# Queries and keys handed over head dimension first in a fused attention and two-layer feed-forward kernel

## The chip, the cores and the metric

The kernel runs on one core of a Trainium2 chip. The metric is device microseconds (us) of one execution. Five engines work at once, each in the order of its own queue: TensorE (PE for its matmuls, PEld for its weight loads), VectorE (DVE), ScalarE (ACT), GpSimd (POOL) and SyncE (SP), which here only issues transfers. Matmul results land in PSUM banks, everything else lives in SBUF.

## The reference, cut to what matters

```python
# q, k, v: (8 batches, 8 heads, 576 positions, 64)
k_p = k.reshape(B, H, 72, 8, 64).mean(axis=3)      # groups of 8 keys are averaged
v_p = v.reshape(B, H, 72, 8, 64).mean(axis=3)
scores = scale * q @ k_p.T                         # 576 x 72 for each head
attn = softmax(scores)
x = (attn @ v_p), heads side by side               # 4608 tokens x 512
x = (h * cos(h)) @ moe_w_out,              h = x @ moe_w_in      # 512 -> 2048 -> 512
x = (g * clip(g + 3, 0, 6) / 6) @ moe2_w_out, g = x @ moe2_w_in
```

## The kernel before

**Attention.** Work is cut into 40 units: 8 batches by 5 units of 128 query rows (the fifth has 64). Heads go in four pairs, so that a pair fills 128 partitions (2 x 64). The keys of a batch are loaded key group by key group (`load_kv`, tile `raw`, one buffer that keys and values share), pooled on DVE with two halvings (L413) and a last addition that is done twice, side by side (L417, tile `kp`). `make_kbd` turns `kp` around with five TensorE transposes (four at L427, one at L443) into a PSUM piece, and five ACT copies (L424) put the result into `kbd`, an operand with the two heads of a pair on its block diagonal; there are two of these, for odd and even batches. A unit's queries are loaded row by row (`load_q`, tile `qm`, four buffers) and turned around in `unit_q` with four transposes (L472) and one ACT copy (L474) into `qT`. Then `unit_s` multiplies `qT` by `kbd`, half of the heads at a time (L486), DVE takes the row maxima (L495) and subtracts them (L497), ACT takes exponentials (L502), DVE and POOL normalise (L508 to L514), `unit_pt` transposes the weights on TensorE (L538), and `pv` multiplies by the pooled values (L573) and stores to `x_d`.

**PSUM.** Attention's PSUM results are "pieces" (`piece`). Up to the point where the first batch's output is complete, scores use the ring `ap` (two buffers), the turned queries and keys use the banks `h`, and the rest uses the banks `y`. After that, every kind of piece takes turns in the ring `ap`.

**First feed-forward layer.** Its 4608 tokens go in nine blocks of 512. A step is one block by one chunk of hidden units: `gemm1` (12 matmuls, L281), a chain of ACT and DVE operations, and two steps later `gemm2` (12 matmuls, L324). x arrives from `x_d` and is split by ACT and POOL (L258, L259). The scores of the first nine units come before any step; the rest is interleaved with the steps. `attention()` is a generator, and each `yield` ends one piece of work; how many pieces have been taken by each half step is fixed by a formula of `base`, `PACE` and the table `GOFF`, and a scheduler orders each engine's queue from that. The last scores are computed near 420 us; then come the rest of the first layer and the second layer (L900).

```python
            if n < units:
                unit_s(n, 0)
                yield
                unit_s(n, 1)
                unit_exp(n)
                yield
```

Of the kernel before, what the change touches and what calls it, by code (L numbers as in the profile page):

```python
# [8 lines left out]
F32 = mybir.dt.float32  # L9
# [3 lines left out]
AF = mybir.ActivationFunctionType  # L13
ALU = mybir.AluOpType
# [4 lines left out]
POOL = 8  # L19
# [9 lines left out]
@with_exitstack  # L29
def tile_kernel(ctx, tc, q, k, v, wi1, wo1, wi2, wo2, ident_d, mask_d, out):  # L30
    nc = tc.nc
    B, H, S, D = q.shape
    DM, NT = out.shape
    P = 128
    N = 512
    SP = S // POOL
    NP = H // 2
# [11 lines left out]
    K0S = 5  # L49
# [6 lines left out]
    KD = [0, 1, 1, 1, 1, 1, 1, 1]  # L56
    VD = [1, 0, 1, 1, 1, 1, 1, 1]
# [6 lines left out]
    KC = (H * SP + P - 1) // P  # L64
    KFULL = (H * SP) // P
    KREM = H * SP - KFULL * P
    UNITS = [(n0, min(P, S - n0)) for n0 in range(0, S, P)]
    NU = len(UNITS)
# [276 lines left out]
    ap = actx.enter_context(tc.tile_pool(name="ap", bufs=1))  # L345
    ps_a = actx.enter_context(tc.tile_pool(name="ps_a", bufs=2, space=PSUM))

    ident = ap.tile([P, P], F32, name="ident")
# [3 lines left out]
    raw, kp = {}, {}  # L352
    kbd = [ap.tile([P, NP, 2 * SP], F32, name=f"kbd{n}") for n in range(2)]
# [3 lines left out]
    qm, qT, pts = {}, {}, {}  # L357
# [7 lines left out]
    def piece(kind):  # L365
        turn = turns[kind] = turns.get(kind, -1) + 1
        if started:
            return ps_a.tile([P, N], F32, tag="ap", name="ap_ps", bufs=2)
        tag = SKIND[kind][turn % len(SKIND[kind])]
        if tag == "ap":  # L370
            return ps_a.tile([P, N], F32, tag="ap", name="ap_ps", bufs=2)
        if tag == "h":
            return ps_h.tile([P, N], F32, tag="h", name="h")
        return ps_y.tile([P, N], F32, tag=tag, name=tag)

    def load_kv(b, nm, step=KFULL):
        src = {"k": k, "v": v}[nm][b].rearrange("h (s r) d -> (h s) (r d)", r=POOL)
        if nm == "v":
            pairs = src.rearrange("(j x) e -> x j e", x=2 * SP)
            nc.sync.dma_start(out=raw_t[:, :NP, :], in_=pairs[:P])  # L380
            for half in range(2):
                o = half * NP * VR
                nc.sync.dma_start(
                    out=raw_t[o : o + NP * VR, NP, :],
                    in_=src.rearrange("(j x) e -> j x e", x=2 * SP)[:, P:],
                )
            return
        for c in range(0, KFULL, step):
            nc.sync.dma_start(
                out=raw_t[:, c : min(c + step, KFULL), :],  # L390
                in_=src[c * P : min(c + step, KFULL) * P, :].rearrange("(c p) e -> p c e", p=P),
            )
        nc.sync.dma_start(out=raw_t[:KREM, KFULL, :], in_=src[KFULL * P :, :])

    def load_q(n):
        b, i = divmod(n, NU)
        n0, w = UNITS[i]
        t = ap.tile([P, H * D], F32, tag="qm", name="qm", bufs=4)
        nc.sync.dma_start(
            out=t[:w].rearrange("p (h d) -> p h d", d=D),  # L400
            in_=q[b, :, n0 : n0 + w, :].rearrange("h p d -> p h d"),
        )
        qm[n] = t

    def pool_kv(b, nm, eng, step=KC):
        kt = ap.tile([P, KC, 2, D], F32, tag="kp", name="kp") if nm == "k" else None
        vt = ap.tile([P, KC, D], F32, tag="vt", name="vt") if nm == "v" else None
        for c in range(0, KC, step):
            t = raw_t[:, c : min(c + step, KC)]
            w = POOL * D  # L410
            while w > 2 * D:
                w //= 2
                eng.tensor_tensor(  # L413
                    out=t[:, :, :w], in0=t[:, :, :w], in1=t[:, :, w : 2 * w], op=ALU.add
                )
            for o in [kt[:, c : min(c + step, KC), e] for e in range(2)] if nm == "k" else [vt[:, c : min(c + step, KC)]]:
                eng.tensor_tensor(out=o, in0=t[:, :, :D], in1=t[:, :, D : 2 * D], op=ALU.add)  # L417
        kp[b, nm] = kt if nm == "k" else vt

    def make_kbd(b, part):  # L420
        kt = kp[b, "k"]
        ps = piece("q")
        kb = kbd[b % 2]
        cp = lambda o, i_: nc.scalar.activation(out=o, in_=i_, func=AF.Copy)  # L424
        if part == 0:
            for c in range(KFULL):
                nc.tensor.transpose(  # L427
                    ps[:, c * P : (c + 1) * P], kt[:, c].rearrange("p e d -> p (e d)"), ident
                )
            full = (KFULL * P) // (2 * SP)  # L430
            cp(
                kb[:D, :full, :SP],
                ps[:D, : full * 2 * SP].rearrange("p (j x) -> p j x", x=2 * SP)[:, :, :SP],
            )
            cp(
                kb[D:, :full, SP:],
                ps[D:, : full * 2 * SP].rearrange("p (j x) -> p j x", x=2 * SP)[:, :, SP:],
            )
            o = full * 2 * SP
            cp(kb[:D, full, :SP], ps[:D, o : o + SP])  # L440
            cp(kb[D:, full, SP : KFULL * P - o], ps[D:, o + SP : KFULL * P])
        else:
            nc.tensor.transpose(  # L443
                ps[:, :KREM], kt[:KREM, KFULL].rearrange("p e d -> p (e d)"), ident[:KREM, :KREM]
            )
            cp(kb[D:, NP - 1, 2 * SP - KREM :], ps[D:, :KREM])

    def make_v(b):
        vt = kp.pop((b, "v"))
# [6 lines left out]
        for x, src, rows in (("h", f(sp_h), P), ("l", sp_l, half)):  # L456
# [7 lines left out]
                in1=rest[:rows].to_broadcast([rows, NP, D]),  # L464
                op=ALU.mult,
            )

    def unit_q(n):
        w = UNITS[n % NU][1]
        ps = piece("q")  # L470
        for j in range(NP):
            nc.tensor.transpose(ps[:, j * P : j * P + w], qm[n][:w, j * P : (j + 1) * P], ident[:w, :w])  # L472
        t = ap.tile([P, NP, P], F32, tag="qT", name="qT", bufs=2)
        nc.scalar.activation(  # L474
            out=t[:, :, :w], in_=ps.rearrange("p (j n) -> p j n", n=P)[:, :, :w], func=AF.Copy
        )
        qT[n] = t
        del qm[n]

    def unit_s(n, half):  # L480
        b, i = divmod(n, NU)
# [104 lines left out]
    def attention():  # L586
        units = B * NU
        normed = finished = 0
        for n in range(units + 3):
            b, i = divmod(n, NU)  # L590
# [6 lines that stand above are left out]
                if n + 3 < units:  # L597
                    load_q(n + 3)
                if n + 1 < units:
                    unit_q(n + 1)  # L600
                    yield
            if n < units and b + 1 < B:
                if i == 2:
                    pool_kv(b + 1, "k", nc.vector if KD[b + 1] else nc.gpsimd)
                    load_kv(b + 1, "v")
                if i == 4:
                    make_kbd(b + 1, 0)
                    yield
                    make_kbd(b + 1, 1)
                    yield  # L610
            while normed < units and n - normed >= NL[normed // NU]:
                unit_norm(normed)
                normed += 1
            while finished < normed and n - finished >= 2:
                unit_pt(finished)
                yield
                qb, qi = divmod(finished, NU)
                finished += 1
                if qi in (1, 3):
                    unit_pt_rest(qb, qi - 1)  # L620
                    yield
                for part, (u0, u1) in enumerate(PARTS[qb]):
                    if qi == min(u1 - 1 + (part == 0) * PV0, NU - 1):
                        for j in range(NP):
                            pv(qb, part, j)
                            yield
                        if UNITS[u1 - 1][0] + P >= N:
                            started.append(qb)
                if qi == NU - 1:
                    done.append(qb)  # L630
                    if qb + 1 < B:
                        pool_kv(qb + 1, "v", nc.vector if VD[qb + 1] else nc.gpsimd)
                        make_v(qb + 1)
                        if qb + 2 < B:
                            load_kv(qb + 2, "k")
# [9 lines left out]
        steps += [(0, (1, bl), bl, fc, fc == n, fc == NF - 1) for fc in range(n, NF)]  # L645
    SB = len(steps)

    load_kv(0, "k", KFULL if K0S > KFULL else K0S)
    nc.sync.dma_start(out=ident, in_=ident_d)
    for n in range(3):  # L650
        load_q(n)
    nc.vector.memset(raw_t[KREM:, KFULL, :], 0.0)
    for n in range(2):
        nc.vector.memset(kbd[n], 0.0)
    nc.sync.dma_start(out=mask[:, : 2 + NP], in_=mask_d)
    for t in vr.values():
        nc.gpsimd.memset(f(t), 0.0)
    pool_kv(0, "k", nc.vector, K0S)
    load_kv(0, "v")
    make_kbd(0, 0)  # L660
    make_kbd(0, 1)
    unit_q(0)
    pool_kv(0, "v", nc.vector if VD[0] else nc.gpsimd)
    make_v(0)
    load_kv(1, "k")
    att = attention()
# [441 lines left out]
```

## Time and profile before

| | us |
|---|---|
| median of three runs (lowest, highest) | 1718.68 (1715.75, 1719.0) |
| the profiled execution, its own time | 1720.11 |
| its span, first to last instruction | 1718.3 |
| PE busy in the span | 1648.3 |
| DVE busy | 1158.8 |
| ACT busy | 981.3 |
| POOL busy | 346.4 |

Busy time of PE counts overlapping matmuls once. The span is the profiled execution alone, so the sums of the prediction stand against 1720.11 us, and their difference is taken off the median.

### The profile page before, as it was taken

How to read it: one execution, taken by the hardware profiler on the slowest of the kernel's cores; microseconds unless marked ns; L12 is line 12 of the kernel's file. 1: busy time of each engine (PE TensorE's matmuls, PEld its weight loads, DVE VectorE, ACT ScalarE, POOL GpSimd, SP SyncE). 2: the span in 40 equal slices, each digit the busy share in tenths (PEclk: the TensorE clock that was granted, in tenths of full speed). 3: DMA queues.
4: the chain of work that ended last, by engine and by line, in shares of the span. 5: the costliest groups of instructions: out<-in, count | busy, mean ns of one | idle time of the engine just before them, and what ended most of it. 6: DMA issues, size and time to landing. Idle time of an engine off the chain costs nothing. (4 is left out here: it accounts for less than half of the span.)

```text
span 1718.3 us, 21588 instructions
## 1 busy us (share of the span) xinstructions
PE 1648.3 (96%) x7858; PEld 1368.2 (80%) x7858; DVE 1158.8 (67%) x1580; ACT 981.3 (57%) x1473; POOL 346.4 (20%) x266
## 2 busy tenths in 40 slices
PE   4789999999999999999999998999999999999999
PEld 3567777787888888888888788888888888888889
DVE  6999666656676888788887435353555576768665
ACT  3578887788666666666565434353444344444444
POOL 2756543232333201111104003020202000000000
PEclk8799999999999999999999998999999999999999
DMA  7756434321433367656566274243428955344231
GB/s 189 217 170 184 151 121 126 113 87 35 150 115 129 93 206 267 195 188 206 184 209 189 99 283 145 99 167 128 147 114 302 324 224 187 113 157 137 84 110 38
DMA packets 174857, 274.11 MB, mean 160 GB/s; under 512 B 48672, under 2 KB 95904, under 8 KB 174752
## 3 DMA queue, kind: packets, MB, share of 16 engines
q1 hardware_dynamic: 174752, 272.75, 48.3%
q8 instruction: 62, 1.02, 0.3%
q14 instruction: 43, 0.35, 0.1%
HBM read 167.84 MB, written 104.86 MB: 159 GB/s over the span
## 5 line engine op out<-in xcount | busy, mean ns | idle before, releaser
L900 PE MATMUL bank<-wa,wb 128*128 128x512 f32 (+1 forms) x1368 | 292.8, 362 | 5.7 <-issue 4.1
L900 PEld LDWEIGHTS bank<-wa,wb 128*128 128x128 f32 x1368 | 235.4, 193 | 44.2 <-issue 4.2
L324 PE MATMUL y<-gh,wb 128*128 128x512 f32 x648 | 211.8, 391 | 0.0
L281 PE MATMUL h<-xh,wb 128*128 128x512 f32 x648 | 211.6, 390 | 0.2 <-ACT xh L258 0.2
L752 ACT ACTIVATE wa<-wu 128x1024 fp32r<-128x1024 f32 (+1 forms) x130 | 127.5, 981 | 142.7 <-PE bank L900 124.4
L900 PE MATMUL bank<-wu,wb 128*128 128x512 f32 (+1 forms) x792 | 198.4, 386 | 0.0
L294 DVE SCALAR_TENSOR_TENSOR g<-g,t 128x512 f32<-128x512 f32 x144 | 116.4, 809 | 102.4 <-ACT g L293 101.8
L281 PE MATMUL h<-xh,wa 128*128 128x512 f32 x504 | 175.0, 404 | 0.0
L259 POOL TENSOR_TENSOR xl<-xr,xh 128x512 fp32r<-128x512 f32 x72 | 107.6, 1508 | 324.0 <-ACT xh L258 323.3
L900 PEld LDWEIGHTS bank<-wu,wb 128*128 128x128 f32 x792 | 148.8, 188 | 29.9
L324 PE MATMUL y<-gh,wa 128*128 128x512 f32 x504 | 169.6, 396 | 0.0
L324 PEld LDWEIGHTS y<-gh,wb 128*128 128x128 f32 x648 | 122.4, 189 | 25.5
L281 PEld LDWEIGHTS h<-xh,wb 128*128 128x128 f32 x648 | 121.6, 188 | 25.6 <-ACT xh L258 0.6
L297 ACT ACTIVATE g<-g 128x512 f32<-128x512 f32 x144 | 91.1, 633 | 72.3 <-DVE g L294 71.9
L304 ACT ACTIVATE gh<-g 128x512 fp32r<-128x512 f32 x144 | 90.5, 629 | 68.7 <-DVE g L301 68.3
L281 PE MATMUL h<-xl,wb 128*128 128x512 f32 x324 | 126.3, 390 | 1.1 <-POOL xl L259 1.1
L753 DVE TENSOR_TENSOR wa<-wu,wa 128x1024 fp32r<-128x1024 f32 (+1 forms) x80 | 89.5, 1124 | 55.3 <-ACT wa L752 55.2
L324 PE MATMUL y<-gl,wb 128*128 128x512 f32 x324 | 126.5, 390 | 0.0
L301 DVE TENSOR_TENSOR g<-h,g 128x512 f32<-128x512 f32 x144 | 98.8, 686 | 36.8 <-ACT g L297 36.6
L1011 ACT ACTIVATE wu<-bank,bias_c 128x1024 f32<-128x1024 f32 (+1 forms) x60 | 61.8, 1031 | 99.2 <-PE bank L900 85.4
L900 PE MATMUL bank<-wa,wa 128*128 128x512 f32 (+1 forms) x552 | 117.5, 359 | 0.0
L288 ACT ACTIVATE t<-h 128x512 f32<-128x512 f32 x144 | 84.9, 590 | 52.8 <-PE h L281 52.3
(174 smaller groups left out, 3101.4 us busy)
## 6 DMA issues: line engine op xcount, KB each, us to landing
g_d<-wu SPq DMA_DIRECT2D x64, 512.0 KB, 2.6
wu<-g_d SPq DMA_DIRECT2D x56, 512.0 KB, 4.5
xr<-x_d SPq DMA_DIRECT2D x72, 256.0 KB, 3.3
wb<-s_d SPq DMA_DIRECT2D x36, 512.0 KB, 5.0
s_d<-wa SPq DMA_DIRECT2D x32, 512.0 KB, 3.7
s_d<-wa SPq DMA_DIRECT2D x32, 384.0 KB, 4.5
yp_d<-ys SPq DMA_DIRECT2D x36, 256.0 KB, 2.3
yv<-yp_d SPq DMA_DIRECT2D x36, 256.0 KB, 3.5
```

Source lines behind the costliest of these rows:

```text
L259: nc.gpsimd.tensor_tensor(out=xl, in0=t, in1=f(xh), op=ALU.subtract)
L281: nc.tensor.matmul(h, a[:, cs], z, start=(n == 0), stop=(n == 3 * NC - 1))
L288: nc.scalar.activation(out=t, in_=hs[s], func=AF.Copy, bias=0.25, scale=INV_2PI)
L294: mark[s] = nc.vector.scalar_tensor_tensor(out=g, in0=g, scalar=MAGIC, in1=t, op0=ALU.subtract, op1=ALU.subtract)
L297: nc.scalar.activation(out=g, in_=g, func=AF.Sin, scale=-TWO_PI)
L301: nc.vector.tensor_tensor(out=g, in0=hs[s], in1=g, op=ALU.mult)
L304: nc.scalar.activation(out=gh, in_=g, func=AF.Copy)
L324: nc.tensor.matmul(y[c], a, z, start=(first and n == 0), stop=(last and n == 2))
L752: nc.scalar.activation(out=hi, in_=src, func=AF.Copy)
L753: el.tensor_tensor(out=lo, in0=src, in1=f(hi), op=ALU.subtract)
L900: nc.tensor.matmul(bank[:, e, :wide], w[:, j, h, e], z[:, j], start=start and j == 0 and x == 0, stop=stop and j == 1 and x == 2, skip_gro ...
L1011: nc.scalar.activation(out=r, in_=c, func=AF.Relu, bias=bias_c[:, 2:3], scale=1.0)
```

## The change

The host hands over `q` as (batch, head pair, 2 x 64, 576) and `k` as (batch, 2 x 64, 8 x 4 x 72), with the position inside a key group outermost. So a query load lands directly as `qT`, now with four buffers, and `unit_q`, `qm` and the second tile are gone. The keys land with the head dimension on the partitions; `pool_k` halves them twice over 2304 elements (L407 of the new kernel) and does the last addition as two DVE operations of 64 partitions that write the two diagonal blocks of `kbd` (L411). `make_kbd` and `kp` are gone. The values' path, the number of yields and all pacing tables stay; a yield that ended a `unit_q` or `make_kbd` piece now ends an empty one. The reordering on the host is not part of the time.

```diff
-        for c in range(0, KFULL, step):
-            nc.sync.dma_start(
-                out=raw_t[:, c : min(c + step, KFULL), :],
-                in_=src[c * P : min(c + step, KFULL) * P, :].rearrange("(c p) e -> p c e", p=P),
-            )
-        nc.sync.dma_start(out=raw_t[:KREM, KFULL, :], in_=src[KFULL * P :, :])
+        flat = raw_t.rearrange("p c e -> p (c e)")
+        for c in range(0, POOL, step):
+            cs = slice(c * NP * SP, (c + step) * NP * SP)
+            nc.sync.dma_start(out=flat[:, cs], in_=k[b][:, cs])
...
-        t = ap.tile([P, H * D], F32, tag="qm", name="qm", bufs=4)
+        t = ap.tile([P, NP, P], F32, tag="qT", name="qT", bufs=4)
         nc.sync.dma_start(
-            out=t[:w].rearrange("p (h d) -> p h d", d=D),
-            in_=q[b, :, n0 : n0 + w, :].rearrange("h p d -> p h d"),
+            out=t[:, :, :w], in_=q[b, :, :, n0 : n0 + w].rearrange("j p n -> p j n")
         )
-        qm[n] = t
+        qT[n] = t
...
+    def pool_k(b, eng):
+        t = raw_t.rearrange("p c e -> p (c e)")[:, : POOL * NP * SP]
+        w = POOL * NP * SP
+        while w > 2 * NP * SP:
+            w //= 2
+            eng.tensor_tensor(out=t[:, :w], in0=t[:, :w], in1=t[:, w : 2 * w], op=ALU.add)
+        t = t.rearrange("p (r j x) -> p r j x", j=NP, x=SP)
+        kb = kbd[b % 2]
+        for e, p in enumerate((slice(0, D), slice(D, P))):
+            eng.tensor_tensor(
+                out=kb[p, :, e * SP : (e + 1) * SP], in0=t[p, 0], in1=t[p, 1], op=ALU.add
+            )
...
                 if n + 1 < units:
-                    unit_q(n + 1)
                     yield
             if n < units and b + 1 < B:
                 if i == 2:
-                    pool_kv(b + 1, "k", nc.vector if KD[b + 1] else nc.gpsimd)
+                    pool_k(b + 1, nc.vector)
                     load_kv(b + 1, "v")
                 if i == 4:
-                    make_kbd(b + 1, 0)
                     yield
-                    make_kbd(b + 1, 1)
                     yield
```

What that makes of the queues shows at three places. First, the beginning of PE's queue, before (`kp` pooled keys, `qm` queries as loaded, `e` the scores less their maxima, `y` a PSUM bank):

```order
L427 MATMUL h<-ident,kp 128x128 x4
L443 MATMUL h<-ident,kp 128x64
L472 MATMUL h<-ident,qm 128x128 x8
L486 MATMUL ap_ps<-kbd_104,qT 128x144 x4
L472 MATMUL h<-ident,qm 128x128 x4
L486 MATMUL ap_ps<-kbd_104,qT 128x144 x6
L538 MATMUL y_280<-ident,e_106 128x128
```

And the same place in the changed kernel, where scores are L452 and the transposes of the weights L504 and L526:

```order
L452 MATMUL ap_ps<-kbd_104,qT 128x144 x12
L504 MATMUL y_235<-ident,e_106 128x128 x4
L452 MATMUL ap_ps<-kbd_104,qT 128x144 x4
L504 MATMUL y_274<-ident,e_107 128x128 x4
L526 MATMUL y_281<-ident,e_106 128x128
```

The score matmuls of three units now stand first, with nothing of PE or ACT between the pooled keys and them. Second, the beginning of DVE's queue before, after its first memsets:

```order
L413 TENSOR_TENSOR raw<-raw 128x5x256
L413 TENSOR_TENSOR raw<-raw 128x5x128
L417 TENSOR_TENSOR kp<-raw 128x5x64 x2
L495 TENSOR_REDUCE mx<-ap_ps 128x4 x2
L497 TENSOR_TENSOR e_106<-ap_ps,mx 128x288 x2
L495 TENSOR_REDUCE mx<-ap_ps 128x4
L413 TENSOR_TENSOR raw<-raw 128x5x256
```

And in the changed kernel, where L407 and L411 pool the keys, L461 and L463 are the maxima and the subtraction, and L420 pools the values:

```order
L407 TENSOR_TENSOR raw<-raw 128x1152
L407 TENSOR_TENSOR raw<-raw 128x576
L411 TENSOR_TENSOR kbd_104<-raw 64x4x72 x2
L461 TENSOR_REDUCE mx<-ap_ps 128x4
L463 TENSOR_TENSOR e_106<-ap_ps,mx 128x288
L461 TENSOR_REDUCE mx<-ap_ps 128x4
L463 TENSOR_TENSOR e_106<-ap_ps,mx 128x288
L461 TENSOR_REDUCE mx<-ap_ps 128x4 x2
L463 TENSOR_TENSOR e_107<-ap_ps,mx 128x288 x2
L420 TENSOR_TENSOR raw<-raw 128x5x256
```

The first pooling of values stands behind three more operations of the second unit than before. Third, PE's queue in the middle of the interleaved part, at the same step of the first layer, before:

```order
L324 MATMUL y_1959<-gh,wa_928 128x512
L486 MATMUL ap_ps<-kbd_104,qT 128x144 x2
L324 MATMUL y_1959<-gl,wa_928 128x512
L486 MATMUL ap_ps<-kbd_104,qT 128x144 x2
L324 MATMUL y_1959<-gh,wa_929 128x512
L324 MATMUL y_1960<-gh,wa_928 128x512
L472 MATMUL ap_ps<-ident,qm 128x128 x4
L324 MATMUL y_1960<-gl,wa_928 128x512
```

And in the changed kernel:

```order
L324 MATMUL y_1741<-gh,wa_794 128x512
L452 MATMUL ap_ps<-kbd_104,qT 128x144 x2
L324 MATMUL y_1741<-gl,wa_794 128x512
L452 MATMUL ap_ps<-kbd_104,qT 128x144 x2
L324 MATMUL y_1741<-gh,wa_795 128x512
L324 MATMUL y_1742<-gh,wa_794 128x512
L504 MATMUL ap_ps<-ident,e_106 128x128 x4
L324 MATMUL y_1742<-gl,wa_794 128x512
```

The transposes of queries are gone, the step holds the same scores, and the transposes of the weights (before, four matmuls of L324 later) have moved up into their place in the ring `ap`.

## Rows read from the trace of the kernel before

**Rows 1.** The page, part 1: busy us (share of the span) and instructions.

```profile
PE 1648.3 (96%) x7858; PEld 1368.2 (80%) x7858; DVE 1158.8 (67%) x1580; ACT 981.3 (57%) x1473; POOL 346.4 (20%) x266
```

**Rows 2.** Windows, by stage: start:end, length, busy us by engine, granted clock, DMA share, GB/s.

```profile
20.00:80.00 60.00, 36.94 (x171) 29.01 (x172) 55.91 (x100) 28.52 (x61) 38.07 (x33) 0.72 0.74 202
80.00:160.00 80.00, 67.30 (x356) 52.35 (x355) 76.07 (x123) 63.85 (x118) 46.75 (x39) 0.98 0.60 176
160.00:420.00 260.00, 248.94 (x1320) 201.80 (x1319) 166.24 (x306) 211.71 (x362) 99.89 (x93) 1.00 0.36 110
420.00:1044.00 624.00, 617.78 (x2815) 514.34 (x2813) 457.48 (x681) 375.93 (x623) 116.81 (x79) 0.99 0.54 177
1044.00:1718.00 674.00, 669.78 (x3170) 564.50 (x3170) 396.08 (x357) 296.41 (x302) 43.68 (x18) 1.00 0.44 155
```

**Rows 3.** Groups by line, 0 to 620 us: count, busy us, mean ns, idle before.

```profile
L472 PE MATMUL ap_ps<-ident,qm 128*128 128x128 f32 (+1 forms) x128 | 19.1, 269 | 6.8 <-issue 6.7
L427 PE MATMUL ap_ps<-ident,kp 128*128 128x128 f32 x24 | 3.6, 272 | 0.0
```

**Rows 4.** Windows of line L472 alone (PE, PEld).

```profile
80.00:160.00 80.00, 4.33 (x28) 3.02 (x28) 0.98 0.60 176
160.00:420.00 260.00, 13.22 (x92) 10.07 (x92) 1.00 0.36 110
```

**Rows 5.** Windows of line L427 alone (PE, PEld).

```profile
160.00:420.00 260.00, 2.40 (x16) 1.88 (x16) 1.00 0.36 110
```

**Rows 6.** Timeline of PE near 193 us: start us, length us, what.

```profile
192.69 0.39 PE L281 MATMUL h<-xl,wa 128*128 128x512 f32 x1
192.93 0.60 PE L472 MATMUL ap_ps<-ident,qm 128*128 128x128 f32 x4
193.36 0.60 PE L427 MATMUL ap_ps<-ident,kp 128*128 128x128 f32 x4
193.72 0.48 PE L281 MATMUL h<-xh,wa 128*128 128x512 f32 x1
...
194.26 0.40 PE L324 MATMUL y<-gl,wa 128*128 128x512 f32 x1
194.59 0.27 PE L443 MATMUL ap_ps<-ident,kp 64*128 64x64 f32 x1
194.79 0.50 PE L324 MATMUL y<-gh,wa 128*128 128x512 f32 x1
```

**Rows 7.** Waits of PE, 160 to 420 us: total us, times, longest.

```profile
PE ap_ps L472 <- issue: 3.5, 3, 1.8
PE ap_ps L486 <- DVE pth L551: 2.0, 3, 1.1
PE h L281 <- POOL xl L259: 2.0, 3, 1.0
```

**Rows 8.** Timeline of the start, all engines, in brackets the idle time before.

```profile
7.57 2.35 DVE L413 TENSOR_TENSOR raw<-raw 128x1280 f32<-128x1280 f32 x2 [4.69 <-DMA raw<-in_k_dram]
9.96 0.90 DVE L417 TENSOR_TENSOR kp<-raw 128x320 f32<-128x320 f32 x2
10.88 0.37 SPq L380 DMA_DIRECT2D raw<-in_v_dram  x1
...
15.04 2.29 PE L486 MATMUL ap_ps<-kbd,qT 128*128 128x144 f32 x8
...
16.41 0.46 DVE L495 TENSOR_REDUCE mx<-ap_ps 128x4 f32<-128x288 f32 x1 [5.55 <-PE ap_ps L486]
...
20.92 1.49 DVE L413 TENSOR_TENSOR raw<-raw 128x1280 f32<-128x1280 f32 x1 [1.36 <-DMA raw<-in_v_dram]
```

**Rows 9.** Waits of DVE, 0 to 160 us.

```profile
DVE mx L495 <- PE ap_ps L486: 8.5, 5, 5.6
```

**Rows 10.** Windows 55:65 and 80:130, columns as in rows 2.

```profile
55.00:65.00 10.00, 6.66 (x26) 5.91 (x27) 9.90 (x21) 3.36 (x6) 7.18 (x7) 0.53 0.71 195
80.00:130.00 50.00, 40.78 (x217) 32.52 (x216) 48.51 (x77) 38.09 (x70) 26.93 (x23) 0.97 0.59 169
```

More of the change, by code (lines that the diff above doesn't have):

```diff
@@ L31, in tile_kernel @@
     nc = tc.nc
-    B, H, S, D = q.shape
+    B, H, S, D = v.shape
     DM, NT = out.shape
@@ L374, in piece, with load_kv @@
         return ps_y.tile([P, N], F32, tag=tag, name=tag)
-    def load_kv(b, nm, step=KFULL):
-        src = {"k": k, "v": v}[nm][b].rearrange("h (s r) d -> (h s) (r d)", r=POOL)
+    def load_kv(b, nm, step=POOL):
         if nm == "v":
+            src = v[b].rearrange("h (s r) d -> (h s) (r d)", r=POOL)
             pairs = src.rearrange("(j x) e -> x j e", x=2 * SP)
@@ L397, in load_q @@
         n0, w = UNITS[i]
-        t = ap.tile([P, H * D], F32, tag="qm", name="qm", bufs=4)
+        t = ap.tile([P, NP, P], F32, tag="qT", name="qT", bufs=4)
         nc.sync.dma_start(
-            out=t[:w].rearrange("p (h d) -> p h d", d=D),
-            in_=q[b, :, n0 : n0 + w, :].rearrange("h p d -> p h d"),
-        )
-        qm[n] = t
[L405 to L418, printed above, removed]
@@ L420, in make_kbd @@
-    def make_kbd(b, part):
-        kt = kp[b, "k"]
-        ps = piece("q")
-        kb = kbd[b % 2]
[L424 to L433, printed above, removed]
-            )
-            cp(
-                kb[D:, :full, SP:],
-                ps[D:, : full * 2 * SP].rearrange("p (j x) -> p j x", x=2 * SP)[:, :, SP:],
-            )
[L439 to L446, printed above, removed]
+            out=t[:, :, :w], in_=q[b, :, :, n0 : n0 + w].rearrange("j p n -> p j n")
+        )
@@ L448, in make_v, with pool_v @@
+    def pool_v(b, eng):
+        vt = ap.tile([P, KC, D], F32, tag="vt", name="vt")
+        w = POOL * D
+        while w > 2 * D:
+            w //= 2
+            eng.tensor_tensor(
+                out=raw_t[:, :, :w], in0=raw_t[:, :, :w], in1=raw_t[:, :, w : 2 * w], op=ALU.add
+            )
+        eng.tensor_tensor(out=vt, in0=raw_t[:, :, :D], in1=raw_t[:, :, D : 2 * D], op=ALU.add)
+        kp[b, "v"] = vt
     def make_v(b):
@@ L466, in make_v @@
             )
[L468 to L478, printed above, removed]
     def unit_s(n, half):
@@ L631, in attention @@
                     if qb + 1 < B:
-                        pool_kv(qb + 1, "v", nc.vector if VD[qb + 1] else nc.gpsimd)
+                        pool_v(qb + 1, nc.vector if VD[qb + 1] else nc.gpsimd)
                         make_v(qb + 1)
@@ L646, in tile_kernel @@
     SB = len(steps)
-    load_kv(0, "k", KFULL if K0S > KFULL else K0S)
+    load_kv(0, "k")
     nc.sync.dma_start(out=ident, in_=ident_d)
@@ L651, in tile_kernel @@
         load_q(n)
-    nc.vector.memset(raw_t[KREM:, KFULL, :], 0.0)
     for n in range(2):
@@ L657, in tile_kernel @@
         nc.gpsimd.memset(f(t), 0.0)
-    pool_kv(0, "k", nc.vector, K0S)
+    pool_k(0, nc.vector)
     load_kv(0, "v")
[L660 to L663, printed above, removed]
+    pool_v(0, nc.vector if VD[0] else nc.gpsimd)
     make_v(0)
@@ L1096 @@
     given = {name: _words(_np.ascontiguousarray(inputs[name])) for name in _INS} | _constants()
+    b, h, s, d = given["q"].shape
+    given["q"] = given["q"].reshape(b, h // 2, 2, s, d).transpose(0, 1, 2, 4, 3)
+    given["q"] = _np.ascontiguousarray(given["q"]).reshape(b, h // 2, 2 * d, s)
+    given["k"] = given["k"].reshape(b, h // 2, 2, s // 8, 8, d).transpose(0, 2, 5, 4, 1, 3)
+    given["k"] = _np.ascontiguousarray(given["k"]).reshape(b, 2 * d, h // 2 * s)
     for name, a in given.items():
```

## Prediction

> **What bounds the kernel now.** I read the page's busy shares first, then windows by stage, and only then lines. PE is busy 96% of the span [rows 1], which makes PE the suspect, but an average over stages can hide another limit, and the reader should see in the windows where it does [rows 2]. From 420 us to the end PE is busy 617.8 of 624 and then 669.8 of 674 us [rows 2]: nothing there waits for anything else, and the change touches nothing there, so that this tail keeps its length and only moves. From 160 to 420 us PE is busy 248.9 of 260 us, while ACT has 211.7, DVE 166.2 and POOL 99.9: PE is the limit, and 11.1 us of idle are left in it. From 80 to 160 us it is the other way round: DVE is busy 76.1 of 80 us, PE 67.3. From 20 to 80 us DVE has 55.9 of 60 and PE 36.9, with the clock at 0.72 on average. So PE work that goes away is worth its price behind 160 us, while before that only what shortens DVE's queue, or lets it start earlier, is worth anything. The whole kernel then ends as much earlier as the point near 420 us at which PE becomes saturated.
>
> **What the change removes from PE behind 160 us.** In rows 4 there are 92 query transposes, 23 units of four. What one costs isn't its duration: the mean is 269 ns [rows 3], but consecutive ones overlap. I take the distance between starts on a full PE [rows 6]: four query transposes begin at 192.93 and the next work at 193.36, 0.43 us. The four key transposes take 0.36 us (193.36 to 193.72), the single one 0.20 us (194.59 to 194.79), and 0.09 us before it is lost against the usual distance of 0.24 us (192.69 to 192.93). So 23 x 0.43 = 9.9 us for queries, and, with four batches in the stretch [16 transposes, rows 5], 4 x 0.65 = 2.6 us for keys: 12.5 us. Upper bound: the busy times, 13.2 + 2.4 and four times 0.27 us [rows 4 to 6], 16.7 us. The lower bound is the 12.5 itself as long as PE remains the limit; what happens if it doesn't is a rival.
>
> The Trainium skill, "TensorE: Matmul & The Clock Gate", Part 4 on the PE-mode transpose, gives about 275 ns for a transpose inside a kernel. The duration in rows 3 agrees with it (269 to 272 ns); charged for all 200 transposes it would make 55 us (an estimate from that page), and the time 1664 us. The distances of rows 6 say that 0.11 us of each is really occupied, and the sum goes by these.
>
> **Waits on PE behind 160 us.** Of the 11.1 us of idle, 3.5 us stand directly before query transposes [rows 7]. They wait for a buffer of the ring `ap`, held by the first half of the scores until DVE has subtracted the maxima. The order shown for the third place says what is late next: the transposes of the weights move up into the same place in the ring and wait for the same subtraction, only 0.43 us of queue apart. The whole 3.5 us may remain or all may go; I take half, 1.8 us, because a piece less per unit goes through the ring. The other waits (values' and x's low parts, 2.0 us each at most, rows 7) I leave as they are. Behind 160 us: 12.5 + 1.8 = 14.3 us, from 12.5 to 16.7 + 3.5 = 20.2.
>
> **The start.** The pooled keys are ready at 10.86 us, and the first row maximum is taken at 16.41 [rows 8]: DVE sits 5.55 us while keys are turned, copied, queries turned and copied, and scores computed. In the new order only the scores remain of this, 15.04 to 16.41, 1.37 us at the clock of that time. The pooling itself, 3.29 us (7.57 to 10.86), shrinks with its elements, 1152 for 1280, 576 for 640 and 288 for 320, a tenth each: 2.96 us. So the first maximum would come at 7.57 + 2.96 + 1.37 = 11.9 us, 4.5 us earlier. That is the upper bound, since the next stop is not moved by it: the first values, asked for at 10.88 when the keys' buffer is free, are pooled at 20.92 after a wait for their landing. They are now asked for 0.3 us earlier, and land some 0.3 us earlier if the transfers before them take as long. What DVE gains there is this and the three operations that the new order puts ahead of the values, 1.2 us at 0.4 each (the row for 16.41 shows 0.46): 1.5 us is the lower bound. The four later waits for scores, 8.5 - 5.55 = 3.0 us [rows 8, 9], have query transposes before them too. I take 3.0 us for the start, halfway between 1.5 and 4.5.
>
> **DVE until 160 us.** Four more batches' keys are pooled there, each a tenth shorter, 4 x 0.33 = 1.3 us. Of the 4.1 + 3.9 us of DVE's remaining idle in 20 to 160 us [rows 2] I take 1.0 us, as chains that went PE to ACT to PE for each unit are gone; bounds 0 and 4. PE's own savings before 160 us I cost at nothing: DVE covers them. Without that cover the 28 query transposes of 80 to 160 us [rows 4], seven units, would be worth 7 x 0.43 = 3.0 us more. Before 160 us: 3.0 + 1.3 + 1.0 = 5.3 us, from 2.8 to 9.8.
>
> **Costed at nothing.** ACT's copies of queries and keys: ACT has 48 us to spare behind 160 us [rows 2]. Query loads: the same 256 KB in pieces twice as long, with four buffers to land in; they now wait for the scores of the unit four before and have three units to land. The key load: one transfer for two. No wait is added on DVE by writing `kbd` directly, since the `kbd` that is written was last read a batch ago.
>
> **Sum.** 14.3 + 5.3 = 19.6 us off the profiled execution's 1720.1, that is 1700.5; the median of the runs shown is 1.4 us lower, so 1699.
>
> **The rivals.** A measurement of this kernel tells a change from none at about 0.2%, 3.4 us.
>
> (1) The start is swallowed and the ring's waits stay: DVE, in order, stands before the values until they land, and PE's waits come back in front of the weights' transposes. Then only the 12.5 us count: 1706. For it speaks that the values' wait is a transfer's, against it that three DVE operations demonstrably pass ahead. Chance 0.2.
>
> (2) Everything comes: 20.2 + 9.8 = 30 us, 1689. It needs the ring's waits gone and DVE filled without a gap until 160 us. Chance 0.1.
>
> (3) PE stops being the limit behind 160 us. A step shrinks by some 5% there, and PE already waits 7.6 us for DVE, ACT and POOL; if those waits grow by 8 us with attention's chain of maximum, exponential, sum and product, 6 us remain of the 14.3, and with half of the start's, 1710. Against it: DVE is busy 64%, POOL 38%, ACT 81% and loses a share of its own. Chance 0.08.
>
> (4) The other side, by the clock. Below 80 us PE runs at half speed, 1.2 GHz, wherever it has stood idle, as in 55 to 65 us (granted 0.53, busy 6.7 us of 10), and from 80 to 130 us near full speed (0.97) with 40.8 us busy of 50 [rows 10]. Without transposes PE idles more before 80 us. If it then stayed at half speed until 130 us, the 38 us that are left of the 40.8 would take some 74 us instead of 50: 24 us lost against 19.6 gained, 1723. It decides from about 40 us of further half speed on. Against it: of 67.3 us in 80 to 160 only 4.3 are query transposes [rows 2, 4], and the first layer's matmuls come as densely as before. Chance 0.04. The Trainium skill, the same page, Part 1, has the array at 1.2 GHz until sustained matmul work raises it, and Part 4 adds that transposes don't count as such work; by that the rise would not come later, and the price above wouldn't fall due. No row here separates transposes from other work in this.
>
> (5) The transposes lie wholly in time that PE waits anyway: 1718. The 95.7% of rows 2 speak against it. Chance 0.03. (6) Each is worth its full 270 ns: 1664, chance 0.01, against rows 6.
>
> **How the numbers follow.** My forecast, 1699, has the remaining 0.54. Faster by over 3.4 us: forecast, (1), (2), (3), (6), together 0.93. Within 3.4 us: (5), 0.03; slower: (4), 0.04. The range reaches from (2) to (3), 1688 to 1711, which leaves out (4), (5), (6) and the edges of (2) and (3).
>
> **What would show it.** Right: PE's busy time falls by 25 to 35 us in all; the first row maximum near 12 us; DVE waiting for values near 20 us, now for longer; the last scores near 400 us instead of 420; the tail behind them unchanged in length. Wrong: new waits of PE on the weights' transposes of more than 3 us behind 160 us, a granted clock below 0.9 in 80 to 130 us, or DVE idle growing in 20 to 160 us. The prediction would fail most simply if the first values landed later than 20.9 us, or if PE's idle behind 160 us grew by as much as its work shrank.

## The result and the profile after

The changed kernel takes 1702.4 us (median of four runs, 1701.9 to 1703.0), the kernel before 1718.8 beside it: a ratio of 0.9908, 95% interval 0.9892 to 0.9923, 16.4 us less. 1699 was forecast, range 1688 to 1711. The profiled execution went from 1720.1 to 1703.0 us. The size was nearly right, but its two parts were not, as the views show.

The page of the changed kernel, part 1, answers to [rows 1]: PE's busy time fell by 25.5 us, for 200 instructions less.

```profile
PE 1622.8 (95%) x7658; PEld 1349.7 (79%) x7658; DVE 1162.1 (68%) x1579; ACT 952.1 (56%) x1393; POOL 351.1 (21%) x266
```

Its start on DVE answers to [rows 8] (columns as there).

```profile
6.25 2.15 DVE L407 TENSOR_TENSOR raw<-raw 128x1152 f32<-128x1152 f32 x2 [4.09 <-DMA raw<-in_k_dram]
8.44 0.92 DVE L411 TENSOR_TENSOR kbd<-raw 64x288 f32<-64x288 f32 x2
10.78 0.46 DVE L461 TENSOR_REDUCE mx<-ap_ps 128x4 f32<-128x288 f32 x1 [1.42 <-PE ap_ps L452]
...
17.71 1.49 DVE L420 TENSOR_TENSOR raw<-raw 128x1280 f32<-128x1280 f32 x1 [2.35 <-DMA raw<-in_v_dram]
```

The first maximum comes 5.6 us earlier, 1.3 of it because the keys land at 6.25 instead of 7.57 us, and the first values are pooled 3.2 us earlier. Windows by stage answer to [rows 2].

```profile
20.00:80.00 60.00, 33.59 (x140) 25.95 (x140) 53.35 (x97) 23.94 (x49) 37.77 (x34) 0.80 0.61 193
80.00:160.00 80.00, 66.72 (x332) 50.67 (x330) 77.26 (x122) 61.14 (x101) 48.98 (x39) 0.98 0.54 167
160.00:403.00 243.00, 229.31 (x1174) 189.79 (x1174) 169.83 (x302) 191.35 (x314) 102.00 (x92) 0.99 0.37 120
```

Clock times mislead when the work itself shifts. The first layer has 144 steps, and each begins on ACT with one L288, so the start of the nth L288 says how far the kernel has come. Step 8 begins at 164.84 us (before 165.28), step 18 at 251.64 (254.06), step 40 at 424.72 (440.17). So of the start's 5.6 us 3.3 are left at step 0 (83.77 us, before 87.06) and 0.4 at step 8; 2.0 us come between steps 8 and 18, 13.0 between 18 and 40. Behind step 40 the kernels of this study are the same program, and their tails last 1274.6 to 1278.6 us: that is scatter of a single profile, and of the 17.1 us between the two profiles 1.6 belong to it.

Windows from step 8 to step 40 show PE (first columns), of the kernel before and then, for PE alone, of the changed one.

```profile
165.28:440.17 274.89, 264.28 (x1402) 214.78 (x1401) 172.05 (x318) 222.19 (x385) 102.98 (x95) 1.00 0.36 113
```

```profile
164.84:424.72 259.88, 247.71 (x1282) 0.99 0.37 120
```

120 matmuls fewer, 16.6 us of PE work less; idle rose from 10.6 to 12.2 us; together 15.0 us. From step 18 on the split is plainer, here of the kernel before and then of the changed one.

```profile
87.06:254.06 167.00, 151.06 (x801) 119.91 (x800) 133.61 (x227) 137.90 (x246) 92.30 (x82) 0.99 0.51 154
254.06:440.17 186.11, 179.82 (x957) 147.08 (x956) 113.37 (x211) 149.80 (x257) 54.78 (x51) 1.00 0.32 102
```

```profile
83.77:251.64 167.87, 144.42 (x715) 114.19 (x714) 143.54 (x228) 125.66 (x211) 95.91 (x81) 0.97 0.51 159
251.64:424.72 173.08, 169.38 (x891) 141.32 (x890) 113.00 (x212) 142.00 (x234) 57.38 (x53) 1.00 0.33 105
```

In the second row of each PE works 10.4 us less and is idle 3.7 instead of 6.3 us: 13.0. In the first row PE works 6.6 us less and the stretch is 0.9 us *longer*, while DVE is busy 9.9 us more with one instruction more. That line is the puzzle of this case.

A part of it is TensorE's clock. Cut into windows of 10 us, the granted clock between 80 and 260 us is 1.00 but in these, of the kernel before and then of the changed one:

```profile
90.00:100.00 10.00, 7.82 (x43) 6.90 (x41) 10.00 (x15) 7.98 (x15) 5.75 (x5) 0.83 0.27 86
```

```profile
110.00:120.00 10.00, 7.06 (x28) 5.26 (x26) 8.75 (x13) 5.67 (x11) 3.92 (x5) 0.83 0.63 197
160.00:170.00 10.00, 8.30 (x40) 7.41 (x40) 8.94 (x14) 6.56 (x15) 5.63 (x6) 0.83 0.64 214
210.00:220.00 10.00, 7.38 (x28) 5.35 (x26) 7.12 (x14) 4.60 (x6) 3.07 (x3) 0.83 0.19 53
```

There PE falls to the lower of its two levels, 1.2 GHz, for a part of the window: once before, three times now. Each time PE had just waited, 2.2 us in the kernel before, 2.8, 2.5 and (in two pieces) 2.6 us in the changed one. Its first two, on PE:

```profile
113.31 1.16 PE L452 MATMUL ap_ps<-kbd,qT 128*128 128x144 f32 x4 [2.75 <-DVE e L463]
161.70 0.64 PE L539 MATMUL ap_ps<-ptl,vmh 128*128 128x320 f32 x1 [2.54 <-DVE ptl L509]
```

The mean clock of the first row is 0.99 before and 0.97 now; 0.02 of 168 us is some 3 us of PE at full speed (an estimate). So without the clock PE would have worked some 10 us less there, not 6.6. Not every such wait is followed by a fall: behind the one of 3.1 us that ends at 173.19 us, shown further down, the clock stays at 1.00.

### The profile page after: what moved, and what is told of

Same layout as the page of the kernel before. It is cut to its first block, busy times and chain, and to the rows that moved or that the text cites. A ratio compares the mean times of both kernels' runs of the same rounds, so it can differ in the third digit from the quotient of the medians.

```text
span 1701.2 us, 21102 instructions
## 1 busy us (share of the span) xinstructions
PE 1622.8 (95%) x7658; PEld 1349.7 (79%) x7658; DVE 1162.1 (68%) x1579; ACT 952.1 (56%) x1393; POOL 351.1 (21%) x266
## 5 line engine op out<-in xcount | busy, mean ns | idle before, releaser
L324 PE MATMUL y<-gh,wb 128*128 128x512 f32 x648 | 210.8, 389 | 0.0
L294 DVE SCALAR_TENSOR_TENSOR g<-g,t 128x512 f32<-128x512 f32 x144 | 112.4, 781 | 95.0 <-ACT g L293 94.4
L324 PE MATMUL y<-gh,wa 128*128 128x512 f32 x504 | 171.1, 398 | 0.0
L324 PEld LDWEIGHTS y<-gh,wb 128*128 128x128 f32 x648 | 121.7, 188 | 25.3
L324 PE MATMUL y<-gl,wb 128*128 128x512 f32 x324 | 126.0, 389 | 0.0
L281 PEld LDWEIGHTS h<-xh,wa 128*128 128x128 f32 x504 | 95.3, 190 | 23.5 <-issue 2.0
```

Source lines behind the costliest of these rows:

```text
L281: nc.tensor.matmul(h, a[:, cs], z, start=(n == 0), stop=(n == 3 * NC - 1))
L294: mark[s] = nc.vector.scalar_tensor_tensor(out=g, in0=g, scalar=MAGIC, in1=t, op0=ALU.subtract, op1=ALU.subtract)
L324: nc.tensor.matmul(y[c], a, z, start=(first and n == 0), stop=(last and n == 2))
```

## The experiments

Theory 1 was that PE is the limit behind some 240 us and that before it DVE's queue and the waits there swallow what is gained. All kernels below are the changed one or the one before, with the edit shown. Times are medians, each compared with the kernel before in the same session; the intervals of the ratios are about 0.0015 to either side, 2.5 us.

| kernel | us | ratio | step 18 at | step 40 at |
|---|---|---|---|---|
| changed | 1702.4 | 0.9908 | 251.6 | 424.7 |
| q_only | 1701.5 | 0.9895 | 248.4 | 421.8 |
| k_only | 1705.7 | 0.9925 | 246.8 | 427.4 |
| pe_early | 1704.4 | 0.9916 | 252.2 | 424.7 |
| pe_late | 1706.8 | 0.9925 | 250.7 | 430.2 |
| dve_early | 1703.0 | 0.9900 | 252.9 | 425.8 |
| dve_late | 1703.0 | 0.9903 | 249.6 | 423.6 |
| dve_start | 1699.0 | 0.9889 | 248.1 | 420.5 |
| eps_early | 1698.3 | 0.9879 | 246.5 | 419.0 |
| eps_none | 1696.8 | 0.9872 | 249.6 | 422.2 |
| nomax_early | 1693.5 | 0.9858 | 241.0 | 413.9 |
| nomax_all | 1692.8 | 0.9851 | 240.0 | 415.7 |
| nomul_early | 1691.0 | 0.9845 | 241.4 | 414.6 |

The steps are read from one profiled execution of each kernel, which is up to 3.3 us off the median (`dve_early` and `eps_none` above it, `dve_start` 1.5 below), and its granted clock between steps 0 and 18 lies between 0.95 (`pe_early`, `dve_early`) and 0.99 (before, `pe_late`, `eps_early`). So some 3 us more or less at step 18 decide nothing by themselves.

**One half of the change at a time.** `q_only` leaves the keys' loading, pooling and `make_kbd` as before, `k_only` the queries' loading and `unit_q`.

> Only the queries are handed over with the head dimension first; keys are loaded, pooled, transposed and copied as before. It loses 160 of the 200 transposes. Theory 1 (behind some 240 us PE is the limit, before it DVE's queue and the waits there swallow what is gained): the query transposes of units 21 to 39 and the waits ahead of them are all that reaches the end, so most of the changed kernel's 16.4 us: 1704 to 1708 us, 11 to 15 us less than before. Rival (what is gained at the start, by keys that need no transposes and copies, carries to the end): the keys' part is worth 5 us or more, and queries alone give no more than 10 us: 1709 or above.

> Only the keys are handed over with the head dimension first and pooled straight into the block-diagonal operand; queries are loaded, transposed and copied as before. It loses 40 of the 200 transposes and the copies behind them. Theory 1: the early start is lost again until some 220 us, and what reaches the end are three or four groups of key transposes behind 240 us at 0.65 us each, 2.0 to 2.6 us, and what little waits they took with them: 1714 to 1717. Rival (the start carries): 1710 to 1713, 5 us or more below before.

The halves give 17.6 and 13.3 us, together far more than the whole's 16.4. `q_only` came out 2.5 us below theory 1's range. For `k_only` theory 1 was wrong by some 10 us, and the rival, nearer to it, by 4 or more. The windows of `k_only` from step 0 to 18 and 18 to 40:

```profile
81.73:246.84 165.11, 150.20 (x783) 119.19 (x782) 132.84 (x226) 131.83 (x226) 92.99 (x81) 0.98 0.54 164
246.84:427.40 180.56, 177.44 (x947) 146.31 (x946) 112.83 (x212) 148.00 (x247) 55.66 (x51) 1.00 0.32 100
```

It keeps 7.2 us at step 18, where the changed kernel keeps 2.4, and DVE's busy time stays at 132.8 us. Behind step 18 PE's idle falls to 3.1 us with the keys alone. In `q_only` it falls to 2.0 us. So idle was one gain that either half takes, once. That is some 5 us of the overlap between the halves; the larger part lies before step 18, where either half alone keeps more (7.2 and 5.6 us) than both together (2.4). The 56 query transposes that `k_only` still has there cost 177.44 - 169.38 = 8.1 us of PE, 0.58 for a group of four.

**PE work put back.** Four transposes of the query tile a unit, with nothing behind them, in units 1 to 19 or 21 to 39:

```diff
+    def ballast(n):
+        w = UNITS[n % NU][1]
+        ps = piece("q")
+        for j in range(NP):
+            nc.tensor.transpose(ps[:w, j * P : (j + 1) * P], qT[n][:, j, :w], ident)
...
                 if n + 1 < units:
+                    if n + 1 < 20:        # pe_late: n + 1 > 20
+                        ballast(n + 1)
                     yield
```

> The changed kernel with ballast: for each of units 1 to 19 (scored until some 215 us) four transposes of the query tile on PE, into the same ring place as the removed ones, with nothing behind them; they begin 0.11 us apart, so 0.43 us a unit, 8.2 us of PE work in all. Theory 1 (until some 220 us PE has time to spare): 0 to 2 us slower than the changed kernel, 1702 to 1705. Rival (PE work counts from 160 us on or everywhere): the share of units 12 to 19 at least, 3.4 us, up to 8.2: 1706 to 1711.

> The changed kernel with the same ballast of four transposes for each of units 21 to 39 (scored from some 220 us to 403 us), nothing for the others: again 8.2 us of PE work. Theory 1 (PE is the limit there and every transpose counts by its distance of 0.11 us): 8 to 9 us slower than the changed kernel, 1710 to 1712; more than that, up to 1716, if the waits for a place in the ring come back with them. Rival (the gain came from ACT's copies, the loads or the start, not from PE): 0 to 3 us slower, 1702 to 1705. If a transpose is worth its duration of 0.27 us: 20 us slower, 1723.

Early, the median rises by 2.0 us, within the interval, and step 40 comes no later (424.7 in both). Late, it rises by 4.4 us, half of what was expected, and the five executions spread widely, 1703.8 to 1708.7. In the profiled one, the slowest of the five, the stretch from step 18 to 40 grew from 173.1 to 179.5 us:

```profile
250.70:430.21 179.51, 177.02 (x947) 148.52 (x946) 112.76 (x212) 142.69 (x233) 55.42 (x52) 0.99 0.31 101
```

56 of the 76 transposes lie there: 7.6 us of PE, 6.4 us of length, 0.11 each. Up to some 2 us of both is the clock's (0.99 there, 1.00 in the changed kernel; an estimate, 0.01 of 179.5 us). The other 20 lie before step 18, which comes no later.

**DVE work added.** Theory 2 put DVE's queue in the place of the limit until some 215 us. `scr` is a scratch tile; these additions go into `pool_k`, ahead of the pooling:

```diff
+        for n in range(4 if b in (1, 2, 3) else 0):   # dve_late: 6, b in (6, 7); dve_start: 6, b == 0
+            eng.tensor_tensor(out=scr, in0=t[:, : w // 4], in1=t[:, w // 4 : w // 2], op=ALU.add)
```

> The changed kernel with four more additions of 128x576 on DVE, into a scratch tile, ahead of the pooling of each of the key batches 1, 2 and 3 (between 29 and 117 us): twelve operations at some 0.74 us (the 128x576 halving's usual duration in the changed kernel), 8.9 us of DVE work. Theory 2 (until some 215 us DVE's queue sets the pace, whatever PE has to do there; behind 240 us PE does): 5 to 9 us slower than the changed kernel, 1707 to 1711. Rival (what happens before 215 us is made up later, because PE waits between 240 and 280 us anyway, 3 us of 40): 0 to 3 us slower, 1702 to 1705.

> The changed kernel with six more such additions ahead of the pooling of key batches 6 and 7 (from some 209 us and some 269 us on): again 8.9 us of DVE work. Theory 2: 0 to 2 us slower than the changed kernel, 1702 to 1704, since DVE has 13 to 15 us of each 40 to spare there. Rival (DVE's queue delays attention's chain, and PE waits): 4 to 9 us slower, 1706 to 1711.

> The changed kernel with six additions of 128x576 into a scratch tile ahead of the first batch's key pooling: 6 x 0.73 = 4.4 us, so that the first row maximum comes near 15.2 us instead of 10.8, much as before the change. If the earlier start is worth what the prediction gave it (3 us): 1705 to 1707, 3 to 4.4 us slower than the changed kernel. If it is swallowed later (the values land when they land, and DVE's queue behind them sets the pace): 0 to 1.5 us slower, 1702 to 1704.

None of the three made the kernel measurably slower. For the late one that was theory 2's forecast; the early one refutes it as stated: 8.9 us more in DVE's queue, nothing in the median. And the start isn't shown to be worth anything: with it put back, the kernel came out at 1699.0 us, 3.4 us below the changed one and outside both forecasts; the intervals of the two ratios overlap. Of `dve_start`, on DVE (pooling is L410 there, the maximum L464):

```profile
10.78 1.36 DVE L410 TENSOR_TENSOR raw<-raw 128x1152 f32<-128x1152 f32 x1
...
16.15 0.45 DVE L464 TENSOR_REDUCE mx<-ap_ps 128x4 f32<-128x288 f32 x1
```

The first maximum is back at 16.15 us, all but where it was before the change [rows 8], yet step 18 comes no later than in the changed kernel (248.1 for 251.6 us, granted clock 0.98 for 0.97).

**DVE work taken away.** `eps_early` drops one operation of 8 elements (on each partition) in units 0 to 19, `eps_none` in all. The sum there is at least 1, and 1e-9 added to it is lost in the rounding of fp32, so this is a version to keep; that the outputs agree to the last bit is argued, not shown. The nomax kernels leave out maxima and subtraction, and ACT takes the exponentials straight from the scores:

```diff
-        nc.vector.tensor_scalar(out=sm[:w], in0=sm[:w], scalar1=1e-9, scalar2=None, op0=ALU.add)
+        if n >= 20:                # eps_none: never
+            nc.vector.tensor_scalar(out=sm[:w], in0=sm[:w], scalar1=1e-9, scalar2=None, op0=ALU.add)
```

```diff
+        if n < 20:                 # nomax_all: n < 40; unit_exp returns at once for these
+            e = ebuf[n % NE][:w, half * 4 * SP : (half + 1) * 4 * SP]
+            nc.scalar.activation(
+                out=e, in_=ps[:w, : 4 * SP], func=AF.Exp, scale=1.0 / (math.sqrt(D) * POOL)
+            )
+            return
```

> The changed kernel without the addition of 1e-9 to the sums of the exponentials in units 0 to 19 (a sum is at least 1 there, since the maximum is subtracted first). It is one DVE operation of 8 elements a unit, 0.17 us alone, up to 1.27 us in the changed kernel's trace, 0.46 us on average, so 9 us of DVE work less until some 212 us. Theory 2 (DVE sets the pace there): 3 to 8 us faster than the changed kernel, 1694 to 1699. Rival (made up or lost later, or the time is that of the neighbour on GpSimd and passes to the next DVE operation): within 2 us of the changed kernel, 1700 to 1704.

> The same without the addition in all 40 units. Theory 2: the same as without it in units 0 to 19, within 1.5 us, since DVE isn't what PE waits for behind 240 us: 1693 to 1699. Rival (DVE's chain counts late too): another 2 to 4 us faster than with the early units alone.

> The changed kernel, where units 0 to 19 leave out the maxima and their subtraction on DVE, and ACT takes the exponentials straight from the scores, in two halves instead of one piece (softmax without the shift; the scores of these inputs are small). DVE loses 40 maxima and 40 subtractions at 0.45 us, 36 us of work until some 212 us; ACT gains 20 instructions; PE's work stays. Theory 2 (DVE's queue sets the pace until some 250 us, and PE sits idle behind it: 23.5 us between steps 0 and 18, 84 to 252 us): a good part of this idle goes, 8 to 20 us faster than the changed kernel, 1682 to 1694. Rival (the lost time there is a matter of the order, the clock or the loads, not of DVE's work): within 4 us, 1698 to 1706.

> The same for all 40 units. Theory 2: 0 to 4 us beyond the kernel with the early units alone, since PE is idle for only 3.7 us behind 252 us, whatever DVE saves there (another 36 us of DVE work). Rival (DVE's share counts late as much as early): another 8 us or more.

Early units give 4.2 and 8.9 us, the late ones 1.5 and 0.7 more, within the interval. So behind step 18 DVE's work doesn't count, as theory 2 has it, and before it counts, but for 36 us of work taken away only 9 came back. Both edits also shorten each unit's own chain, and no run tells this from a shorter queue. Of `eps_early` and then of `nomax_early`, from step 0 to 18:

```profile
85.53:246.52 160.99, 139.53 (x713) 111.25 (x712) 132.74 (x216) 122.63 (x209) 90.66 (x79) 0.99 0.54 168
```

```profile
83.49:240.98 157.49, 140.56 (x695) 111.79 (x694) 119.70 (x180) 126.13 (x216) 85.46 (x75) 0.97 0.55 171
```

In `eps_early` PE's idle falls by only 2.0 us, from 23.5 to 21.5; the rest is PE being busy 4.9 us less with two matmuls fewer, at a clock of 0.99 for 0.97. In `nomax_early`, at the changed kernel's clock, the idle falls by 6.5 us.

**GpSimd beside DVE.** Theory 3 came from single rows. On DVE and then on POOL, the changed kernel near 40 us:

```profile
39.32 1.36 DVE L127 TENSOR_SCALAR a<-st 128x512 uint32<-128x512 uint32 x1
40.61 0.44 DVE L463 TENSOR_TENSOR e<-ap_ps,mx 64x288 f32<-64x288 f32 x1
40.97 3.02 DVE L131 SCALAR_TENSOR_TENSOR a<-st,a 128x512 uint32<-128x512 uint32 x1
43.92 0.44 DVE L461 TENSOR_REDUCE mx<-ap_ps 64x4 f32<-64x288 f32 x1
```

```profile
39.06 1.34 POOL L478 TENSOR_TENSOR e<-e,sm 128x576 f32<-128x576 f32 x1 [5.13 <-DVE sm L476]
40.37 3.08 POOL L420 TENSOR_TENSOR raw<-raw 128x1280 f32<-128x1280 f32 x1
```

L131 usually takes 0.69 us. Here it lasts 3.02, until 0.5 us behind the end of POOL's L420. The one-line views of L463 (20 to 252 us) and L475 (whole span) give least, median and greatest duration in ns:

```profile
L463 DVE TENSOR_TENSOR e<-ap_ps,mx x46: 437/446/459, 22.3 to 246.3; 128x288 f32<-128x288 f32 x36, 64x288 f32<-64x288 f32 x10
```

```profile
L475 DVE TENSOR_SCALAR sm<-sm x40: 125/175/1267, 20.5 to 410.2; 128x8 f32<-128x8 f32 x32, 64x8 f32<-64x8 f32 x8
```

L463, whose large operand lies in PSUM, never stretches. L475 works on 8 elements: of the 40, 25 with POOL idle took 0.13 to 0.18 us, 15 beside a POOL operation 0.92 on average. The Trainium skill, "SBUF — State Buffer", section "SBUF: two separate sides", says why: DVE and GpSimd share a pair of SBUF ports as an exclusive lock held for a whole instruction, which DVE needs for an instruction with two SBUF inputs or in a mode that uses two ports. The rows agree: L131 ends only behind POOL's operation, and L463, with one input in PSUM, is never late. In which mode L475 runs, no row shows. Counting every DVE operation over 0.1 us longer than the lower quartile of its own form as held up, DVE lost 30 us to this between steps 0 and 18 in the changed kernel, all of it beside POOL operations, and 21 in the kernel before and in `k_only`. That 9 us is the extra busy time of the puzzle. How it reaches PE, at 169 us on DVE, POOL and then PE:

```profile
168.99 0.45 DVE L461 TENSOR_REDUCE mx<-ap_ps 128x4 f32<-128x288 f32 x1
169.35 3.33 DVE L420 TENSOR_TENSOR raw<-raw 128x640 f32<-128x640 f32 x1
172.60 0.45 DVE L463 TENSOR_TENSOR e<-ap_ps,mx 128x288 f32<-128x288 f32 x1
```

```profile
168.48 1.06 POOL L439 TENSOR_TENSOR vrl<-spl,mask 64x256 fp32r<-64x256 f32 x1
169.50 1.27 POOL L310 TENSOR_TENSOR gl<-g,gh 128x512 fp32r<-128x512 f32 x1
170.74 1.25 POOL L145 TENSOR_TENSOR wa<-a,wa 128x512 fp32r<-128x512 f32 x1
```

```profile
173.19 0.63 PE L504 MATMUL ap_ps<-ident,e 128*128 128x128 f32 x4 [3.12 <-DVE e L463]
```

The values' pooling, 0.82 us elsewhere, is held up behind three POOL operations, the subtraction stands behind it, and PE waits for the ring place that the subtraction frees. Ahead of PE's waits at 113 and 161 us, behind which the clock fell, DVE operations were held up too: L136 took 1.54 us at 110.64 (usually 0.68), L294 1.09 us at 160.22 (usually 0.69), both beside POOL. The third, at 213 us, follows DVE's wait for keys to land. The last run takes POOL work away; it leaves out the multiplication by the reciprocal sum:

```diff
-        eng.tensor_tensor(out=e, in0=e, in1=sm[:w].to_broadcast([w, H, SP]), op=ALU.mult)
+        if n >= 20:
+            eng.tensor_tensor(out=e, in0=e, in1=sm[:w].to_broadcast([w, H, SP]), op=ALU.mult)
```

> The changed kernel, where units 0 to 19 leave out the multiplication by the reciprocal sum on GpSimd (their weights stay unnormalised); DVE's and PE's instructions are the same. In the changed kernel's trace those are 24 us of GpSimd's work between 84 and 252 us, and DVE operations that read SBUF through both operands last until the GpSimd operation beside them has ended (an addition of 8 elements 0.17 us with GpSimd idle, 0.92 us on average beside it). Theory 3 (the gain before 252 us was lost to DVE operations held up by GpSimd): DVE's busy time between steps 0 and 18, 143.5 us now, falls by 5 to 10 us with the same instructions, and the kernel gets 3 to 6 us faster than the changed one, 1696 to 1699. Rival (held-up time is absorbed like DVE's extra additions were): within 1.5 us, 1701 to 1704.

```profile
78.58:241.44 162.86, 144.30 (x715) 114.32 (x714) 135.70 (x227) 125.16 (x212) 74.32 (x67) 0.97 0.52 164
```

With PE's instructions unchanged (715) and one fewer of DVE's, DVE's busy time fell from 143.5 to 135.7 us, as expected (by the count above, 23 us lost for 30), and PE's idle from 23.5 to 18.6, at the same granted clock. The kernel gained 11.5 us, twice the forecast: 5.2 of it came ahead of step 0 (78.58 for 83.77 us). The edit also takes the multiplication's own time out of each unit's chain and out of POOL's queue; which of the two gave how much isn't told apart.

## Why the prediction was nearly right, step by step

**PE's work behind 160 us** was undersized: 12.5 us forecast, 16.6 measured from step 8 on, at the upper bound of 16.7; at one clock it would be some 2 us more (0.99 now, 1.00 before; an estimate). The mechanism held. A group of four query transposes is worth 0.58 us there (`k_only`), not 0.43, and the keys' five about 1.0 (`q_only` has ten more than the changed kernel and 2.0 us more of PE), not 0.65. Distances in one place of a full queue [rows 6] were too small a sample; the duration of 0.27 us [rows 3] stays too large.

**The waits behind 160 us**, 1.8 us of gain forecast, became 1.6 us of loss. Waits of PE, 160 to 403 us, answer to [rows 7]:

```profile
PE ap_ps L504 <- DVE e L463: 4.6, 2, 3.1
PE ap_ps L539 <- DVE ptl L509: 2.5, 1, 2.5
PE ap_ps L452 <- DVE ptl L509: 2.2, 2, 1.6
```

The transposes of the weights wait for the subtraction, as the forecast said they could, and over its mark of 3 us. That the 3.5 us of the kernel before were waits for the ring was an inference: rows 7 put them down to "issue", which names no releaser. Both terms together: 15.0 us for 14.3. That this is so near is luck: one was 4.1 us too small, the other 3.4 too large.

**Before 160 us** lies the step that failed: 5.3 us forecast, 0.4 measured at step 8. What was to be seen at the start was seen, and more. But it was taken as a gain that DVE, being the limit, would carry on. The runs show that no queue of the changed kernel carried it: 4.4 us put in at the start, 8.9 us put on DVE and 8.2 us on PE early all vanished in the medians. DVE at 77 of 80 us looked like a full queue, but its busy time holds time held up by POOL, which grew where the gain should have been. DVE's idle between 20 and 160 us grew by 1.4 us instead of shrinking by 1.0. And of the PE work that went away before step 18 the clock took back some 3 us.

**The other signs.** PE's busy time fell by 25.5 us (25 to 35 forecast); DVE waits longer for the values, 2.35 us for 1.36; the last scores come at 404.9 us for 420.1; the tail kept its length within its scatter. The values were asked for at 7.64 instead of 10.88 us, which the forecast had put at 0.3 us.

**The rivals.** (1) is in mechanism what happened, a swallowed start with the ring's waits back; it lay at 1706 only because PE's term was too small in it as well. (3) had PE's waits growing by 8 us; they grew by 1.6. (4) had the clock at half until 130 us; it was 0.98 from 80 to 160, yet it did fall three times instead of once between steps 0 and 18, a price of some 3 us and not 24. (5) and (6) fall with the 16.6 us.

What stays open: why the order in the changed kernel meets POOL more often than in `k_only`, how the lost gain divides between DVE's held-up time and the clock, and whether other executions show the same falls of the clock. The scheduler reorders the queues with each edit, and no run held the order fixed.

## What to carry to other kernels

Split a gain by the stage in which it arises, and let it count only where one engine is really without idle; in a stage where queues wait for each other, test with ballast before believing that an earlier start is worth anything. Read the granted clock in fine windows: the mean of a stage hides short falls. A busy share is not work: compare the busy time of the same instructions in two traces, and look for single durations far above the form's median. And where two edits remove the same idle, their gains don't add.

## What was not expected of the hardware

A DVE operation of 8 elements takes 0.17 us alone and up to 1.27 beside GpSimd; dropping it in 20 units gave 4.2 us, in all 40 units 5.7 us, so that `eps_none`, at 1696.8 us, beats both kernels with, by that arithmetic, the same result in fp32.
